# A retention layer with a gated feed-forward on one Trainium2 core: warm-up matmuls recut, the first slices of block 1 reordered, one store per rest pair

## The chip, the core and the metric

The kernel runs on one core of a Trainium2 chip. A core has a matrix engine (TensorE, PE in the profile), a vector engine (VectorE, DVE), a scalar engine (ScalarE, ACT), GpSimd (POOL) and a sync engine (SP). POOL and SP issue the DMA transfers here: POOL all loads, SP all stores and the transposes done by DMA. The metric is device microseconds of one execution, lower is better. The medians below are over several executions.

## What is computed

Eight batches, eight heads, 576 positions, head dimension 64. The attention-like part has no softmax: the score of positions i >= j is multiplied by a decay `gamma_h ** (i - j)`. Its output, 4608 tokens by 512, goes through a two-layer feed-forward with a gated activation:

```python
scores = scale * np.matmul(q, k.transpose(0, 1, 3, 2))
gamma = 1.0 - 2.0 ** (-5.0 - np.arange(H))
Dmat = np.where(rel >= 0, gamma[:, None, None] ** rel[None, :, :], 0.0)
ret = np.matmul(scores * Dmat[None], v)            # 8 x 8 x 576 x 64
x = ret.transpose(0, 2, 1, 3).reshape(B * S, H * D)  # 4608 x 512
h = x @ w_in                                        # 4608 x 2048
g = h * np.clip(h + 3.0, 0.0, 6.0) / 6.0
out = g @ w_out                                     # 4608 x 512
```

## The kernel before

**Pieces and blocks.** The first 512 positions of each batch are cut into four pieces of 128; the last 64 positions of two batches together make a "rest" piece of 128. Pieces are numbered in the order of work: 0 to 3 are batch 0, 4 to 7 batch 1, 8 to 11 batch 2, 12 the first rest piece. The feed-forward works in nine blocks of 512 tokens: block b holds the main positions of batch b, block 8 the four rest pieces. For each piece the kernel makes transposed q and k (`qk`), the masked scores (`at`), the output `o` out of an "inter" part (the state of earlier pieces) and an "intra" part (within the piece), and copies `o` into `xt16` (`intra`, lines 344 to 353). It also updates a running state: `update_mm` on PE (line 355), then `update_state` (line 372), which is two VectorE operations (`ta`, `ts`, lines 383 and 384) and two ScalarE copies of `ts` into `tbd` (lines 394 and 395).

**First layer.** For each of 16 columns fc of `w_in`, `g1` (line 423) takes one of four PSUM banks of the tag `ph`, runs four matmuls of 128x512 into it (line 409), and `g1_act` (line 412) turns it into `gt`: a ScalarE activation into `u` (line 416), then a VectorE operation (line 417) that reads `u` and the bank. The bank is free for column fc + 4 only after that VectorE operation.

**Second layer.** For each 128 tokens mc, `g2` (line 461) runs 16 matmuls into one bank, a ScalarE copy takes it to `osb` (line 471), and `store` (line 450) issues the store on SP. A block of a batch is one transfer of 128 rows; the last block has rows of two batches in each `osb`, and `store` issues two transfers of 64 rows (line 457). The very last 128 tokens go through `g2_halves` (line 474): two halves of 256 columns, each copied by ScalarE (line 484) and stored.

**Order.** Every engine's order is written out by hand. Small operations can be put off in the list `later`; `run_later(n)` issues the first n. `put` (line 583) issues units of feed-forward work, calls `run_later(1)` after each, and then the steps that a table lists for that unit. `gemm1(kb, steps)` does this for the first layer of block kb.

**The start.** While the first loads come in, `warm` (line 170) gives PE matmuls of zeros: 9 of 128x512 at line 178, then in `transposes_early` (line 206) 6 of 128x512 for piece 0, 8 of 128x128 for each of pieces 1 to 3, between the transposes of k and those of q.

**Block 1.** At lines 613 to 618 the first four banks of block 1 are filled in slices of tokens, because the last pieces of batch 1 are still being made. `g1_columns` (line 428) runs tokens 0 to 255 for all four banks; `second_half(7)` makes the output and the state update of piece 7; then tokens 256 to 383 for all four banks, `ahead(8)`, and tokens 384 to 511 for all four banks, each bank's `g1_act` behind its last matmul. `ahead(c)` (line 539) issues the loads up to piece c + 4 on POOL, the DMA transpose of k, one VectorE operation that scales q and v (`vs`, line 306), and the DMA transpose of the scaled q (line 303). `gemm1(1, ...)` then does columns 4 to 15, with `ahead(9)`, `ahead(10)` and `ahead(11)` after columns 6, 9 and 12. The scores of pieces 8 and 9 (lines 316 and 552) follow on PE.

Of the kernel before, what the change touches and what calls it, by code (L numbers as in the profile page):

```python
# [17 lines left out]
def kernel(  # L18
# [16 lines left out]
    nc = tc.nc  # L35
    B, H, S, D = q.shape
    NTOK, DM = out.shape
    DFF = moe_w_in.shape[1]
    P = 128
    NPAIR = H // 2  # L40
    HALF = P // 2
    NCC = DM // P
    NFC = DFF // P
    MBLK = 512
    NMB = NTOK // MBLK
    MAIN = MBLK
# [19 lines left out]
    def column_of(c):  # L66
        kind, b, i, _ = pieces[c]
        return b * MAIN + i * P if kind == "main" else B * MAIN + b * P
# [8 lines left out]
    win16 = big.tile([P, NCC, DFF], FP16)  # L77
    wout16 = big.tile([P, NFC, DM], FP16)
    xt16 = big.tile([P, NCC, NTOK], FP16)
# [90 lines left out]
    def warm(n, cols):  # L170

        w = psum.tile([P, MBLK], FP32, tag="ph", bufs=4, name=f"warm_{warmed[0]}")
        warmed[0] += 1
        for _ in range(n):
            nc.tensor.matmul(w[:, 0:cols], zeros[:, 0:P], zeros[:, 0:cols],
                             start=True, stop=True)

    warm(9, MBLK)

    mask_rest = const.tile([P, P], FP16)  # L180

# [9 lines left out]
    later = []  # L191
# [14 lines left out]
    def transposes_early(c, alone=True):  # L206
        kn, q16 = loaded[c]["kn"], loaded[c]["q16"]
        qk = work.tile([P, 2, NPAIR, P], FP16, tag="qk", bufs=6, name=f"qk_{c}")
        st[c]["qk"] = qk
        pk = psum.tile([P, NPAIR, P], FP16, tag="ph", bufs=4, name=f"trk_{c}")  # L210
        for p in range(NPAIR):
            nc.tensor.transpose(pk[:, p, :], kn[:, 2 * p:2 * p + 2, :], ident16)
        nc.scalar.copy(qk[:, 1], pk)
        if c == 0:
            warm(6, MBLK)
        elif alone:
            warm(8, P)
        pq = psum.tile([P, NPAIR, P], FP32, tag="ph", bufs=4, name=f"trq_{c}")
        for p in range(NPAIR):
            for h2 in range(2):  # L220
                r = slice(h2 * HALF, h2 * HALF + HALF)
                nc.tensor.matmul(pq[r, p, :], q16[:, 2 * p + h2, :], dq[:, 2 * p + h2, :],
                                 start=(p == 0), stop=(p == NPAIR - 1), skip_group_check=True)
        nc.scalar.copy(qk[:, 0], pq)  # L224
        if c == 0:
            warm(8, P)
# [97 lines left out]
    def inter(c, tag="o"):  # L324
        kind, b, i, _ = pieces[c]
        o = psum.tile([P, NPAIR, P], FP32, tag=tag, bufs=4 if tag == "ph" else 1, name=f"o_{c}")
        st[c]["o"] = o
        st[c]["first"] = True
        if kind == "main" and i == 0:
            return  # L330
        qk = st[c]["qk"]
        if kind == "main":
            states = [(st[c].get("before", state_of[b]), slice(0, P))]
        else:
            states = [(state_of[2 * b], slice(0, HALF)), (state_of[2 * b + 1], slice(HALF, P))]
        for j, (state, cols) in enumerate(states):
            for p in range(NPAIR):
                nc.tensor.matmul(o[:, p, cols], tbd[state][:, p, :], qk[:, 0, p, cols],  # L338
                                 start=(j == 0 and p == 0), stop=False, skip_group_check=True)
            if kind == "rest" or st[c].get("last_reader"):  # L340
                free_tbd.append(state)
        st[c]["first"] = False

    def intra(c):
        o, at, vs = st[c]["o"], st[c]["at"], st[c]["vs"]
        for p in range(NPAIR):
            for h2 in range(2):
                r = slice(h2 * HALF, h2 * HALF + HALF)
                nc.tensor.matmul(o[r, p, :], vs[:, 2 * p + h2, :], at[:, h2, p, :],  # L349
                                 start=(st[c]["first"] and p == 0), stop=(p == NPAIR - 1),  # L350
                                 skip_group_check=True)
        g0 = column_of(c)
        nc.scalar.copy(xt16[:, :, g0:g0 + P], o)  # L353

    def update_mm(cs):

        cs = [c for c in cs if pieces[c][0] != "rest"]
        if not cs:
            return
        u = psum.tile([P, len(cs), NPAIR, D], FP32, tag="tu", name=f"u_{cs[0]}")  # L360
        for j, c in enumerate(cs):
            kn, vs = loaded[c]["kn"], st[c]["vs"]
            st[c]["u"] = u[:, j]
            for p in range(NPAIR):
                for h2 in range(2):
                    r = slice(h2 * HALF, h2 * HALF + HALF)
                    nc.tensor.matmul(u[r, j, p, :], kn[:, 2 * p + h2, :], vs[:, 2 * p + h2, :],  # L367
                                     start=(j == 0 and p == 0),
                                     stop=(j == len(cs) - 1 and p == NPAIR - 1),
                                     skip_group_check=True)  # L370
# [26 lines left out]
    def finish(c):  # L397
        intra(c)
        update_mm([c])
        update_state(c)  # L400
        st.pop(c - 2, None)
        loaded.pop(c)
# [9 lines left out]
    def g1_act(kb, ph, fc):  # L412
        if kb not in gts:
            gts[kb] = work.tile([P, NFC, MBLK], FP16, tag="gt16", bufs=2, name=f"gt16_{kb}")
        u = work.tile([P, MBLK], FP32, tag="moeu", bufs=3, name=f"u_{kb}_{fc}")
        nc.scalar.activation(u, ph, ACTF.Relu, bias=cb[:, 0:1], scale=1.0 / 6.0)  # L416
        nc.vector.scalar_tensor_tensor(out=gts[kb][:, fc, :], in0=u, scalar=1.0,  # L417
                                       in1=ph, op0=ALU.min, op1=ALU.mult)

    def g1_bank(kb, fc):  # L420
        return psum.tile([P, MBLK], FP32, tag="ph", bufs=4, name=f"ph_{kb}_{fc}")
# [3 lines left out]
        g1_mm(kb, ph, fc, range(NCC))  # L425
        g1_act(kb, ph, fc)

    def g1_columns(kb, banks, cols):

        t0 = kb * MBLK  # L430
        for fc, ph in enumerate(banks):
            for dmc in range(NCC):
                nc.tensor.matmul(ph[:, cols], win16[:, dmc, P * fc:P * fc + P],
                                 xt16[:, dmc, t0 + cols.start:t0 + cols.stop],
                                 start=(cols.start == 0 and dmc == 0),
                                 stop=(cols.stop == MBLK and dmc == NCC - 1),
                                 skip_group_check=True)
                if dmc == NCC - 1 and cols.stop == MBLK:
                    g1_act(kb, ph, fc)

    def g1_first(kb):

        banks = [g1_bank(kb, fc) for fc in range(2)]
        for dmcs in ((0, 1), (2, 3)):
            for fc in range(2):
                g1_mm(kb, banks[fc], fc, dmcs)
        for fc in range(2):
            g1_act(kb, banks[fc], fc)

    def store(kb, mc, cols, src):  # L450
        if kb < B:
            r0 = kb * S + P * mc
            nc.sync.dma_start(out[r0:r0 + P, cols], src)
        else:
            for i in range(2):
                r0 = (2 * mc + i) * S + MAIN
                nc.sync.dma_start(out[r0:r0 + HALF, cols], src[i * HALF:i * HALF + HALF])

    pouts = {}

# [13 lines left out]
    def g2_halves(kb, mc):  # L474
        gt = gts[kb]
        W = DM // 2
        for half in range(2):
            pout = psum.tile([P, W], FP32, tag="ph", bufs=4, name=f"pout_{kb}_{mc}_{half}")
            for fc in range(NFC):
                nc.tensor.matmul(pout, gt[:, fc, P * mc:P * mc + P],  # L480
                                 wout16[:, fc, half * W:half * W + W],
                                 start=(fc == 0), stop=(fc == NFC - 1))
            osb = work.tile([P, W], FP32, tag="osh", bufs=2, name=f"osb_{kb}_{mc}_{half}")
            nc.scalar.copy(osb, pout)
            store(kb, mc, slice(half * W, half * W + W), osb)


# [37 lines left out]
    def unit1(kb, f0):  # L525
        return lambda: g1(kb, f0)
# [8 lines left out]
    def second_half(c):  # L535
        inter(c)
        finish(c)
# [58 lines left out]
    def gemm1(kb, steps):  # L596

        units = {0: [lambda: g1_first(kb)]}.get(kb, [])
        done = {0: 2, 1: 4}.get(kb, 0)
        put(units + [unit1(kb, f) for f in range(done, NFC)], steps)  # L600
# [10 lines left out]
    run_later(9)  # L611

    banks = [g1_bank(1, fc) for fc in range(4)]
    g1_columns(1, banks, slice(0, 2 * P))
    second_half(7)
    g1_columns(1, banks, slice(2 * P, 3 * P))
    ahead(8)
    g1_columns(1, banks, slice(3 * P, MBLK))
    gts.pop(0)


    gemm1(1, {2: [(ahead, 9)], 5: [(ahead, 10)], 8: [(ahead, 11)]})
    AT = {1: (-1, 7), 4: (-1, 7, 12), 5: (-1, 3, 7, 11)}
    for kb in range(1, NMB - 1):
        mine, next_ = of_block(kb + 1), of_block(kb + 2)
# [45 lines left out]
```

## Time and profile before

| what | value |
|---|---|
| median of 3 runs | 311.14 us (310.1 to 313.22) |
| profiled execution, its own time | 311.39 us |
| its span, first to last instruction | 309.6 us |
| PE busy | 299.5 us, 97% of the span |
| DVE busy | 185.8 us, 60% |
| ACT busy | 173.6 us, 56% |
| POOL busy | 108.0 us, 35% |

The profile is of one execution. Its own time is 1.8 us above its span: that part lies around the first and the last instruction. "Busy" of PE counts pipelined matmuls, so two neighbours overlap; "PEld" is the load of weights. In rows of the timeline the first two numbers are the start and the length in us, and a bracket at the end gives the idle time before and what ended it. A number in ns is the length of one instruction.

### The profile page before, as it was taken

The page shows a single profiled execution, that of the slowest core. Times are in us where ns is not written, and L with a number is a line of the kernel's source. Part 1 is how long each engine was busy: PE and PEld are TensorE (multiplying, and loading weights), DVE is VectorE, ACT ScalarE, POOL GpSimd, SP SyncE. Part 2 cuts the span into 40 slices and gives each one's busy share as a digit, 9 for nine tenths or more (in the row PEclk, how much of TensorE's full clock was granted, in tenths as well). Part 3 has the DMA queues.
Part 4 walks back from the last instruction along what each step waited for, and adds up shares of the span by engine and source line. Part 5 has one row for each costly group of instructions (what it writes and reads, how often), then busy time and mean ns, then how long its engine had stood idle before and what let it go on. Part 6 is the DMA issues. An engine that isn't in the chain of part 4 may idle for free.

```text
span 309.6 us, 5856 instructions
## 1 busy us (share of the span) xinstructions
PE 299.5 (97%) x2286; PEld 152.6 (49%) x2286; DVE 185.8 (60%) x310; ACT 173.6 (56%) x298; POOL 108.0 (35%) x135
## 2 busy tenths in 40 slices
PE   8889999899999999999999999999999999999994
PEld 3644446544544554445544644455445544444443
DVE  4758715796737882885478737856688357207600
ACT  4657356773457554854574737644765467227611
POOL 8974378696735390045353720130000000000000
PEclk9999999999999999999999999999999999999999
DMA  9999999999999999539998996094423230010033
GB/s 65 145 197 190 204 156 211 168 140 156 191 174 170 114 171 163 118 24 154 146 166 74 140 184 138 17 123 69 104 51 53 83 55 0 34 70 34 1 70 68
DMA packets 153164, 35.52 MB, mean 115 GB/s; under 512 B 143792, under 2 KB 148656, under 8 KB 153136
## 3 DMA queue, kind: packets, MB, share of 16 engines
q0 software_dynamic: 117264, 18.36, 82.9%
q1 hardware_dynamic: 35872, 16.79, 27.6%
q8 instruction: 18, 0.29, 0.4%
q14 instruction: 10, 0.08, 0.1%
HBM read 36.70 MB, written 9.44 MB: 149 GB/s over the span
## 4 chain that ended last, share of the span: by engine, by line
PE 76%; DMA 16%; POOL 6%; issue 1%; DVE 0%; ACT 0%; POOLq 0%
PE pout L467 35%; PE ph L409 31%; DMA wout<-in_moe_w_out_dram 5%; POOL qv L91 4%; DMA win<-in_moe_w_in_dram 3%; DMA qv<-in_v_dram 3%; PE o L349 3%; DMA kn<-in_k_dram 3%; DMA qk<-vs 2%; POOL kn L91 2%; PE o L338 2%; PE sc L316 2%; PE u L367 1%; PE pout L480 1%; PE sc L552 1%
## 5 line engine op out<-in xcount | busy, mean ns | idle before, releaser
L417 DVE SCALAR_TENSOR_TENSOR gt<-u,ph 128x512 f16<-128x512 f32 x144 | 98.1, 687 | 69.0 <-ACT u L416 68.3
L467 PE MATMUL pout<-wout,gt 128*128 128x512 f16 x560 | 126.6, 380 | 0.0
L409 PE MATMUL ph<-xt,win 128*128 128x512 f16 x560 | 122.3, 379 | 1.4 <-DVE gt L417 1.4
L416 ACT ACTIVATE u<-ph,cb 128x512 f32<-128x512 f32 x144 | 98.5, 687 | 25.9 <-PE ph L409 25.4
L409 PEld LDWEIGHTS <-win 128*128 128x128 f16 x560 | 54.7, 98 | 67.3 <-issue 1.6
L467 PEld LDWEIGHTS <-gt 128*128 128x128 f16 x560 | 52.3, 98 | 60.8
L91 POOL DMA_DIRECT2D kn<-in_k_dram x40 | 34.4, 861 | 80.9 <-PE u L367 59.2
L471 ACT COPY osb<-pout 128x512 f32<-128x512 f32 x35 | 20.5, 585 | 48.1 <-PE pout L467 47.8
L91 POOL DMA_DIRECT2D qv<-in_q_dram x40 | 34.2, 858 | 7.4 <-DMA wout<-in_moe_w_out_dram 3.0
L320 DVE TENSOR_TENSOR at<-sc,mask_wide 128x1024 f16<-128x1024 f32 x19 | 23.2, 1223 | 22.4 <-PE sc L316 22.4
L91 POOL DMA_DIRECT2D qv<-in_v_dram x40 | 34.6, 868 | 3.2 <-DMA wout<-in_moe_w_out_dram 1.7
L394 ACT COPY tbd<-ts 64x256 f16<-64x256 f16 x28 | 11.3, 405 | 34.1 <-DVE ts L384 17.2
L353 ACT CAST xt<-o 128x512 f16<-128x512 f32 x35 | 19.3, 588 | 10.9 <-PE o L349 10.7
L306 DVE TENSOR_TENSOR vs<-qv,gqv 128x1024 f16<-128x1024 f16 x28 | 17.9, 684 | 0.0
L560 DVE TENSOR_TENSOR at<-sc,mask_wide 128x512 f16<-128x512 f32 x24 | 15.4, 681 | 0.0
L349 PE MATMUL o<-at,vs 128*64 128x128 f16 x280 | 12.2, 223 | 0.0
L395 ACT COPY tbd<-ts 64x256 f16<-64x256 f16 x28 | 11.2, 401 | 0.4
L383 DVE TENSOR_TENSOR ta<-u,ts 128x256 f32<-128x256 f32 x21 | 8.7, 416 | 3.6 <-PE u L367 3.6
L316 PE MATMUL sc<-qk 64*128 64x128 f16 x184 | 9.1, 218 | 1.2 <-ACT qk L224 1.1
L338 PEld LDWEIGHTS <-tbd 128*128 128x128 f16 x124 | 7.9, 98 | 4.5
L384 DVE TENSOR_TENSOR ts<-ta,gc 128x256 f16<-128x256 f32 x21 | 8.9, 425 | 1.7
L349 PEld LDWEIGHTS <-vs 128*64 128x64 f16 x280 | 8.6, 109 | 2.6 <-issue 0.4
(73 smaller groups left out, 120.1 us busy)
## 6 DMA issues: line engine op xcount, KB each, us to landing
out_dram<-osb SPq DMA_DIRECT2D x32, 256.0 KB, 3.5
kn<-in_k_dram POOLq DMA_DIRECT2D x32, 128.0 KB, 6.2
qv<-in_q_dram POOLq DMA_DIRECT2D x32, 128.0 KB, 6.3
qv<-in_v_dram POOLq DMA_DIRECT2D x32, 128.0 KB, 6.5
wout<-in_moe_w_out_dram POOLq DMA_DIRECT2D x4, 512.0 KB, 15.2
win<-in_moe_w_in_dram POOLq DMA_DIRECT2D x3, 512.0 KB, 10.1
out_dram<-osb SPq DMA_DIRECT2D x6, 128.0 KB, 2.3
win<-in_moe_w_in_dram POOLq DMA_DIRECT2D x2, 256.0 KB, 6.2
```

Of the source, the lines that this page charges most:

```text
L91: nc.gpsimd.dma_start(dst[p0:p0 + n], src[b, :, s0:s0 + n, :].rearrange("h s d -> s h d"))
L306: nc.vector.tensor_tensor(out=vs, in0=qv, in1=gqv, op=ALU.mult)
L316: nc.tensor.matmul(sc[:, h2, p, :], qk[r, 1, p, :], qk[r, 0, p, :], start=True, stop=True)
L320: later.append(lambda: nc.vector.tensor_tensor(out=at.rearrange("t a b s -> t (a b) s"), in0=sc.rearrange("t a b s -> t (a b) s"), in1=mas ...
L349: nc.tensor.matmul(o[r, p, :], vs[:, 2 * p + h2, :], at[:, h2, p, :], start=(st[c]["first"] and p == 0), stop=(p == NPAIR - 1), skip_group ...
L353: nc.scalar.copy(xt16[:, :, g0:g0 + P], o)
L409: nc.tensor.matmul(ph, win16[:, dmc, P * fc:P * fc + P], xt16[:, dmc, t0:t0 + MBLK], start=(dmc == 0), stop=(dmc == NCC - 1))
L416: nc.scalar.activation(u, ph, ACTF.Relu, bias=cb[:, 0:1], scale=1.0 / 6.0)
L417: nc.vector.scalar_tensor_tensor(out=gts[kb][:, fc, :], in0=u, scalar=1.0, in1=ph, op0=ALU.min, op1=ALU.mult)
L467: nc.tensor.matmul(pout, gt[:, fc, P * mc:P * mc + P], wout16[:, fc, :], start=(fc == 0), stop=(fc == NFC - 1))
L471: nc.scalar.copy(osb, pout)
L560: nc.vector.tensor_tensor(out=at[:, h2], in0=banks[h2], in1=mask[:, None, :].to_broadcast([P, NPAIR, P]), op=ALU.mult)
```

## The change

Five edits.

1. The zeros at the start: 36 matmuls of 128x128 in place of 9 of 128x512; for piece 0, 24 of 128x128 in place of 6 of 128x512; for pieces 1 to 3, 2 of 128x512 each in place of 8 of 128x128.
2. Block 1: `g1_columns` does one bank. After tokens 0 to 255 of the four banks come `ahead(8)`, then the output of piece 7 and the PE part of its state update; then the third and fourth slices of the banks are interleaved, so that bank 0 ends after 12 matmuls of 128x128, bank 1 after 20, bank 2 after 28, bank 3 after 32. The state update of piece 7 (VectorE and ScalarE) is put into `later`, behind an empty entry: it is issued after column 5.
3. `ahead(9)` comes after column 4 (it was after column 6), `ahead(10)` after column 8 (it was 9); `ahead(11)` stays after column 12.
4. `store` of the last block: one transfer for the two batches, from a view of `out` with the two batches as its first dimension.
5. `g2_halves`: ScalarE copies the left half of each 256 columns and VectorE the right half.

```diff
-    warm(9, MBLK)
+    warm(36, P)
...
         if c == 0:
-            warm(6, MBLK)
+            warm(24, P)
         elif alone:
-            warm(8, P)
+            warm(2, MBLK)
...
-    def g1_columns(kb, banks, cols):
+    def g1_columns(kb, fc, ph, cols):
         t0 = kb * MBLK
-        for fc, ph in enumerate(banks):
-            for dmc in range(NCC):
-                nc.tensor.matmul(ph[:, cols], win16[:, dmc, P * fc:P * fc + P],
...
-                if dmc == NCC - 1 and cols.stop == MBLK:
-                    g1_act(kb, ph, fc)
+        for dmc in range(NCC):
+            nc.tensor.matmul(ph[:, cols], win16[:, dmc, P * fc:P * fc + P],
...
+        if cols.stop == MBLK:
+            g1_act(kb, ph, fc)
...
         else:
-            for i in range(2):
-                r0 = (2 * mc + i) * S + MAIN
-                nc.sync.dma_start(out[r0:r0 + HALF, cols], src[i * HALF:i * HALF + HALF])
+            rests = out.rearrange("(b s) n -> b s n", s=S)[2 * mc:2 * mc + 2, MAIN:S, cols]
+            nc.sync.dma_start(rests, src)
...
-            nc.scalar.copy(osb, pout)
+            nc.scalar.copy(osb[:, 0:W // 2], pout[:, 0:W // 2])
+            nc.vector.tensor_copy(osb[:, W // 2:W], pout[:, W // 2:W])
...
     banks = [g1_bank(1, fc) for fc in range(4)]
-    g1_columns(1, banks, slice(0, 2 * P))
-    second_half(7)
-    g1_columns(1, banks, slice(2 * P, 3 * P))
+    for fc in range(4):
+        g1_columns(1, fc, banks[fc], slice(0, 2 * P))
     ahead(8)
-    g1_columns(1, banks, slice(3 * P, MBLK))
+    inter(7)
+    intra(7)
+    update_mm([7])
+    third, fourth = slice(2 * P, 3 * P), slice(3 * P, MBLK)
+    for fc, cols in ((0, third), (1, third), (0, fourth), (2, third), (1, fourth), (3, third),
+                     (2, fourth), (3, fourth)):
+        g1_columns(1, fc, banks[fc], cols)
+    later.append(lambda: None)
+    later.append(lambda: update_state(7))
     gts.pop(0)
...
-    gemm1(1, {2: [(ahead, 9)], 5: [(ahead, 10)], 8: [(ahead, 11)]})
+    gemm1(1, {0: [(ahead, 9)], 4: [(ahead, 10)], 8: [(ahead, 11)]})
```

In the changed kernel's program, the VectorE copy of each half in `g2_halves` waits for the ScalarE copy of the same half, and the store for the VectorE copy. On PE the order is otherwise the same, on POOL it is the same.

More of the change, by code (lines that the diff above doesn't have):

```diff
@@ L426, in g1 @@
         g1_act(kb, ph, fc)
-    def g1_columns(kb, banks, cols):
+    def g1_columns(kb, fc, ph, cols):
         t0 = kb * MBLK
-        for fc, ph in enumerate(banks):
-            for dmc in range(NCC):
-                nc.tensor.matmul(ph[:, cols], win16[:, dmc, P * fc:P * fc + P],
[L434 to L437, printed above, removed]
-                if dmc == NCC - 1 and cols.stop == MBLK:
-                    g1_act(kb, ph, fc)
+        for dmc in range(NCC):
+            nc.tensor.matmul(ph[:, cols], win16[:, dmc, P * fc:P * fc + P],
+                             xt16[:, dmc, t0 + cols.start:t0 + cols.stop],
+                             start=(cols.start == 0 and dmc == 0),
+                             stop=(cols.stop == MBLK and dmc == NCC - 1),
+                             skip_group_check=True)
+        if cols.stop == MBLK:
+            g1_act(kb, ph, fc)
     def g1_first(kb):
```

## The prediction

> **What bounds the kernel now.** I read the idle time of PE first, since PE is busy for 97% of the span; then a table of stages, to see where its idle time lies; then the timeline there; then the stores at the end, because the changed stores end the program.
>
> PE's five longest waits (engine, line, who was waited for, total, times, longest):
>
> ```profile
> PE ph L409 <- DVE gt L417: 1.4, 1, 1.4
> PE warm L175 <- DVE cb L112: 1.3, 1, 1.3
> PE sc L316 <- ACT qk L224: 1.1, 2, 0.8
> PE trq L222 <- DMA qv<-in_q_dram: 0.9, 1, 0.9
> PE sc L552 <- DMA qk<-vs: 0.6, 1, 0.6
> ```
>
> Only the first and the last lie in block 1. The table of stages (length, busy time of each engine, then granted clock, DMA share, GB/s):
>
> ```profile
> 53.50:59.50 6.00, 4.56 (x73) 4.09 (x70) 4.01 (x8) 3.95 (x9) 4.71 (x7) 1.00 2.21 175
> 59.50:71.30 11.80, 11.16 (x66) 5.06 (x65) 11.09 (x18) 9.18 (x14) 9.55 (x13) 1.00 2.34 144
> 71.30:290.00 218.70, 218.70 (x1622) 108.27 (x1620) 138.19 (x216) 125.93 (x214) 56.00 (x68) 1.00 0.95 104
> 305.40:309.60 4.20, 0.00 (x0) 0.00 (x0) 0.00 (x0) 0.31 (x1) 0.00 (x0) 1.00 0.22 49
> ```
>
> From 71.3 us on PE never stops until 305.3. So the change can only act before 71.3, where at most some 2 us can be had, and after PE's end, where 4.2 us are left that hold one copy and the last stores. In 59.5 to 71.3 DVE is busy 11.09 of 11.80 us: whatever goes to DVE there is nearly on the path. The timeline of block 1:
>
> ```profile
> 56.05 0.58 ACT L353 CAST xt<-o 128x512 f16<-128x512 f32 x1 [0.94 <-PE o L349]
> 57.17 0.40 ACT L394 COPY tbd<-ts 64x256 f16<-64x256 f16 x1 [0.53 <-DVE ts L384]
> 58.01 3.21 ACT L416 ACTIVATE u<-ph,cb 128x512 f32<-128x512 f32 x5
> 58.73 3.21 DVE L417 SCALAR_TENSOR_TENSOR gt<-u,ph 128x512 f16<-128x512 f32 x5 [1.00 <-ACT u L416]
> 59.47 2.75 PE L409 MATMUL ph<-xt,win 128*128 128x512 f16 x12 [1.44 <-DVE gt L417]
> 64.30 1.19 SPq L303 DMA_TRANSPOSE qk<-vs  x1
> 70.96 0.40 PE L552 MATMUL sc<-qk 64*128 64x128 f16 x8 [0.64 <-DMA qk<-vs]
> ```
>
> PE waits at 58 for bank 0: ACT first made the two state copies, then the activation. At 70.3 it waits for the transposed q of piece 9, issued at 64.30. The stores, first those of 128 rows (L453), then those of 64 (L457), with the table of stages over one store of 128 rows, one pair of 64, and the last pair:
>
> ```profile
> L453 SPq DMA_DIRECT2D out_dram<-osb x32: 332/333/1187, 44.3 to 278.3; - x32
> L457 SPq DMA_DIRECT2D out_dram<-osb x10: 466/562/588, 295.5 to 306.2; - x10
> 250.30:251.20 0.90, 0.90 (x6) 0.42 (x5) 0.64 (x1) 0.72 (x2) 0.00 (x0) 1.00 0.77 291
> 296.70:298.15 1.45, 1.45 (x8) 0.67 (x7) 0.00 (x0) 0.00 (x0) 0.00 (x0) 1.00 0.82 181
> 306.85:307.95 1.10, 0.00 (x0) 0.00 (x0) 0.00 (x0) 0.00 (x0) 0.00 (x0) 1.00 0.53 119
> ```
>
> The share is of 16 DMA engines. A store of 128 rows of 2 KB thus takes 0.77 x 0.90 x 16 = 11.1 engine-us, 87 ns a row; the pair of 64 takes 0.82 x 1.45 x 16 = 19.0, 149 ns a row; the last pair 0.53 x 1.10 x 16 = 9.3 for 128 rows of 1 KB, 73 ns. Same rows, same bytes: how a store is dealt out depends on the pattern that it is written in.
>
> **The zeros at the start: 0.** The 9 matmuls of 128x512 start at 1.26 and the next work at 5.07, 427 ns each. The transposes of k behind them have 128 columns and step at (5.50 - 5.07) / 4 = 107 ns, so 36 x 107 = 3.85 us, as 9 x 427 = 3.84. The 24 for piece 0 cost 24 x 57 = 1.37 us (8 at line 175 take 0.62, a step of 57) for 6 x 216 = 1.30: PE then waits for `dq` until 7.1 in any case. The 2 of 128x512 are 0.02 us shorter than 8 of 128x128. Cover: PE waits 0.86 us for q of piece 3 at 16.44, and all before that may grow by as much. If the clock rose later, 24 x 107 = 2.57 us would end 1.2 us later than now, of which ScalarE's constants and this wait hide nearly all. Bounds -0.1 to +0.4.
>
> **Block 1: +0.3.** Up to 56.07 PE has the same order. Then:
> - Bank 0 ends after 12 matmuls, not after 20. Eight take 8 x 56 = 0.45, to 56.52; the next four need `xt` of piece 7, whose cast ends at 56.63, so PE stops 0.18 and bank 0 ends at 56.92, plus 0.17 until the result is seen. ACT starts at 57.11 (before 58.01: the state copies are gone from ahead of it), 0.69; DVE 57.83 to 58.52; column 4 starts at 58.57, not 59.47: 0.90 gained.
> - ACT and DVE step at 0.63 ((3.21 - 0.69) / 4). ACT does columns 0 to 3 at 57.11, 57.74, 58.37, 59.00, column 4 at 59.63, column 5 at 60.48. DVE: column 4 from 60.35, then `vs` of piece 9 (0.65), column 5 from 61.60 to 62.29, and then the moved state update: `ta` 0.44, a step of 0.08, `ts` 0.43, to 63.2. ACT's next instruction behind column 5 is the state copy, which waits for `ts`; queued behind it is the activation of column 6, whose bank was full at 61.3. The copies run 63.25 to 64.09, so column 6 is seen by DVE at 64.8 and its bank is free at 65.5. Column 10 needs that bank and could start at 63.75: a new wait of 1.8 us, charged to DVE `gt` but made by ACT's queue.
> - After it DVE is back to back: columns 6 to 15 and two `vs`. Columns 4 to 15 end at 70.73 (before 69.82: 59.47 + 12 x 0.864 less rounding). Run with the order of before, the same steps give 64.26, 66.85 and 69.44 for the ends of `vs`, which are the trace's.
> - The transpose of scaled q of piece 9 is issued at 61.7, not 64.30. Landing took 6.5 to 8.8 us in this stage, so it is there by 70.5, and the wait of 0.64 at line 552 goes. Late next: the second bank of those scores needs DVE's column 13 (71.2). State matmuls start at 71.55, not 71.29: +0.26. The other moved transposes: k of 9 goes out at 57.4 for 59.06, q of 8 at 56.1 for 57.76, q of 10 and 11 some 0.5 and 0.9 later; they are needed from 78.9 on and the last, issued at 70.6, is there by 79.4 at the latest, so up to 0.3 late. POOL's order, loads included, is the same.
> Bounds: if ACT did not wait, -1.5; with 0.66 a step in place of 0.63, +0.5.
>
> **The copy in halves: 0.** ACT's copies took 372 ns for 256 columns and 585 for 512, so 265 for 128; DVE about 280 by its 687 for 512 and 416 for 256; one behind the other 0.59 with the hand-over, +0.21. It is on the path only if the stores behind it are not late (below).
>
> **One store per rest pair: +11.1.** No transfer in the trace has a first dimension of 2; all begin with 64 or 128 rows. Lower end: it is dealt over 16 engines like the 128-row store, lands in 2.0 to 2.4 us for 2.1 now and is issued 0.3 sooner: -0.3. Upper end: it is dealt by its first dimension, and two engines move 64 rows each. I take the second, because the two forms in the trace already differ by their pattern alone (87 against 149 ns a row, 333 against 562 ns to issue). One engine alone on its rows is nearest to the 128-row form: 87 ns, so 64 x 87 = 5.57 us a store, and 64 x 43 = 2.75 for a half (73 x 87 / 149 = 43). Three pairs and two halves: 3 x 5.57 + 2 x 2.75 = 22.2 us. The pairs come every 3.45 us (295.55, 299.0, 302.4), less than 5.57, so they queue from the first on. Its data starts at 296.74, +0.26 by block 1, and the last row ends at 297.0 + 22.2 = 319.2. Before, the last row ended at 307.94 and the span 1.66 later; so 320.9, +11.3 with the 0.26. Bounds within this case: 70 ns a row if neighbours overlap on an engine, 13.4 + 4.5 = 17.9, span 316.6; 104 ns (8 rows an engine in 0.83 us of the store at 250.36), 27 us, span 325.6.
>
> The Trainium skill, page "DMA: Bandwidth & Descriptors", section "Why a DMA increments its semaphore by 16 and not by 1", says that the number of DMA engines is the largest up to 16 that divides the slowest dimension of both patterns. Here that is 2, against 16 for every store in the trace; the 16 small packets beside each store's rows agree with the 16, and no run here shows the 2. Its figure of about 27 GiB/s per engine would make an estimate of 4.5 us a store, and a sum near 318.
>
> **Sum.** 309.6 + 0.26 + 11.1 = 320.9 of span; with the 1.8 around it 322.7. The profiled execution (311.39) is 0.25 above the median of the runs, so 322.5.
>
> **Rivals.**
> - The stores go over 16 engines (not slower). For: the bytes are those of a store that lands in 2.0 us now. Against: see above. Then block 1's +0.26 and the end's -0.2 (issue 0.3 sooner, copies 0.2 later, one landing for two) cancel: 311.2. It decides from the point where a pair takes under 3.45 us, that is 54 ns a row on two engines: then nothing queues. Chance 0.13.
> - Two engines, but 149 and 73 ns a row, as in the 64-row form: 3 x 9.5 + 2 x 4.7 = 38 us, span 336.7, time 338.2. Against: there 16 engines were busy with 64 rows at a time, here two are. Chance 0.06.
> - 16 engines, and ACT's wait in block 1 does not cost what I say, since column 10 finds its bank free: 309.3. Against: the order on ACT. Chance 0.03.
>
> **How the numbers follow.** Forecast, two engines at 70 to 104 ns a row: 0.78, time 322.5, from 318 to 327.4. I widen to 317.5 and 329 for the spread of the runs (310.1 to 313.22). About 1% is what a measurement of this kernel can tell from no change: slower by more 0.84 (the forecast and the second rival), within 1% 0.14, faster 0.02.
>
> **What would show it.** Right: the rest stores need 10 us and more to land, the DMA share stays near 2/16 from 297 to 319, PE ends near 305.6. In block 1 PE has one wait of about 0.5 us at column 4, one of 1.8 at column 10, and none for a DMA at the scores of piece 9; ACT is idle 2 us before the state copy in between. Wrong: landings of 2 us, or a PE wait anywhere after 71.5.

## The result and the profile after

The changed kernel took 322.11 us (median of 6 runs, 321.62 to 324.38), the kernel before 310.87 us (its median of six runs; the 311.14 in the table above is that of the first three): a ratio of 1.0365, 95% interval 1.0324 to 1.0406, so 11.3 us more (10.1 to 12.6). The forecast was 322.5 us, with a range of 317.5 to 329.

The profiled execution of the changed kernel is the slowest of its six, 324.38 us with a span of 322.6. It lies 2.3 us above the median for a reason of its own, shown below, at the start.

**The end.** First the DMA view from the first rest store's issue to the end, then the groups of instructions on `osb` there, then the table of stages (length, PE, PEld, DVE, ACT, POOL, then granted clock, DMA share, GB/s), over rest pairs 2 and 3 and over the two halves. The DMA share adds up the times of all packets, so packets that overlap can take it over 1:

```profile
DMA  0010111111111111111111111111111111111000
GB/s 0 0 26 26 30 30 46 40 53 53 50 50 53 53 50 50 53 53 50 50 53 53 50 50 53 53 50 50 50 50 48 48 48 48 50 48 48 33 0 0
DMA packets 650, 1.05 MB, mean 42 GB/s; under 512 B 10, under 2 KB 266, under 8 KB 650
```

```profile
L455 SPq DMA_DIRECT2D out_dram<-osb x5: 511/671/4548, 297.9 to 308.3; - x5
L482 ACT COPY osb<-pout x2: 267/267/267, 305.9 to 307.7; 128x128 f32<-128x128 f32 x2
L483 DVE COPY osb<-pout x2: 292/292/292, 306.2 to 308.0; 128x128 f32<-128x128 f32 x2
```

```profile
305.50:315.76 10.26, 2.15 (x20) 1.68 (x18) 0.58 (x2) 0.53 (x2) 0.00 (x0) 0.85 0.13 51
315.76:321.20 5.44, 0.00 (x0) 0.00 (x0) 0.00 (x0) 0.00 (x0) 0.00 (x0) 0.50 0.14 48
```

The compute engines are done by 308.3, and for 13 us the transfer goes on at a share of 0.13 of 16 engines, which is two. Ten packets are under 512 B: two beside each of the five stores, where the kernel before has sixteen beside each. Two pairs take 10.26 us, so 5.13 a pair and 80 ns a row of 2 KB; the halves take 2.72 each, 42.5 ns a row of 1 KB. The first pair is slower: from 299.15 to 302.95 its rows go at 36 GB/s, which is 114 ns a row on each of two engines, and then at 51.

**Block 1.** PE's waits, and the timeline of ACT, DVE and PE around the moved state update:

```profile
PE ph L409 <- DVE gt L417: 1.9, 2, 1.5
PE trq L222 <- DMA qv<-in_q_dram: 1.7, 1, 1.7
PE warm L175 <- DVE cb L112: 1.3, 1, 1.3
PE sc L316 <- ACT qk L224: 1.1, 2, 0.8
```

```profile
58.45 2.12 PE L432 MATMUL ph<-xt,win 128*128 128x128 f16 x32
59.55 3.21 ACT L416 ACTIVATE u<-ph,cb 128x512 f32<-128x512 f32 x5 [0.53 <-PE ph L432]
61.02 5.34 PE L409 MATMUL ph<-xt,win 128*128 128x512 f16 x24 [0.44 <-DVE gt L417]
...
65.51 0.41 ACT L394 COPY tbd<-ts 64x256 f16<-64x256 f16 x1 [1.89 <-DVE ts L384]
66.36 3.21 ACT L416 ACTIVATE u<-ph,cb 128x512 f32<-128x512 f32 x5
67.08 1.88 DVE L417 SCALAR_TENSOR_TENSOR gt<-u,ph 128x512 f16<-128x512 f32 x3 [1.60 <-ACT u L416]
67.82 4.48 PE L409 MATMUL ph<-xt,win 128*128 128x512 f16 x20 [1.46 <-DVE gt L417]
...
73.64 0.44 PE L367 MATMUL u<-vs,kn 128*64 128x64 f16 x16
```

The one wait of 1.44 before column 4 has become two: 0.44 there, and 1.46 six columns later. The wait for the DMA transpose of piece 9 is gone. Read backwards: PE at 67.82 waits for DVE, DVE for ACT (1.60), ACT for DVE's `ts` (1.89). From the third slice to the state matmuls of pieces 8 and 9 PE takes 15.19 us (58.45 to 73.64), before 15.22 (56.07 to 71.29):

```profile
56.07 1.96 PE L433 MATMUL ph<-xt,win 128*128 128x128 f16 x32
71.29 0.44 PE L367 MATMUL u<-vs,kn 128*64 128x64 f16 x16
```

**The start of this execution.** Block 1 begins 2.38 us late. The table of stages, first of the kernel before, then of the changed one:

```profile
12.00:15.00 3.00, 3.00 (x52) 2.28 (x50) 2.52 (x4) 1.75 (x3) 3.00 (x5) 1.00 2.19 145
15.00:19.20 4.20, 3.14 (x52) 2.23 (x50) 2.88 (x5) 1.90 (x4) 4.11 (x6) 1.00 1.40 183
```

```profile
12.00:15.00 3.00, 1.28 (x16) 0.59 (x14) 1.57 (x2) 0.59 (x1) 2.63 (x5) 1.00 2.35 153
15.00:19.20 4.20, 4.20 (x46) 2.46 (x41) 2.58 (x4) 1.76 (x3) 4.20 (x6) 0.59 1.44 190
```

Here the q of piece 2 came later, PE waited 1.7 us for it, and then the granted clock was 0.59 until 19.2. The experiment with the zeros alone, below, bears on whether that belongs to the change.

### The profile page after: what moved, and what is told of

Its sections match the earlier page's. It is cut to its first block, busy times and chain, and to the rows that moved or that the text cites. A ratio compares the mean times of both kernels' runs of the same rounds, so it can differ in the third digit from the quotient of the medians.

```text
span 322.6 us, 5905 instructions
## 1 busy us (share of the span) xinstructions
PE 301.1 (93%) x2313; PEld 155.7 (48%) x2313; DVE 186.1 (58%) x312; ACT 173.2 (54%) x298; POOL 108.0 (33%) x135
## 4 chain that ended last, share of the span: by engine, by line
PE 88%; DMA 2%; POOL 2%; DVE 2%; ACT 1%; issue 1%; ACTq 0%; POOLq 0%
PE pout L465 38%; PE ph L409 36%; PE o L349 3%; PE sc L316 2%; DMA qv<-in_q_dram 2%; PE o L338 2%; PE u L367 1%; PE pout L478 1%; POOL qv L91 1%; PE ph L432 1%; POOL kn L91 1%; PE sc L551 1%; ACT u L416 1%; DVE gt L417 1%; PE trq L222 1%
## 5 line engine op out<-in xcount | busy, mean ns | idle before, releaser
L394 ACT COPY tbd<-ts 64x256 f16<-64x256 f16 x28 | 11.3, 405 | 35.5 <-DVE ts L384 18.6
L353 ACT CAST xt<-o 128x512 f16<-128x512 f32 x35 | 19.3, 588 | 10.9 <-PE o L349 10.7
```

## The experiments

Each was run beside the kernel before on the same chip; ratios are to that kernel, with 95% intervals. The theory: the store's first dimension of 2 puts it on two DMA engines, and all the rest is near 0. Rivals: a store over two batches is slow in whatever order; block 1, the zeros or the split copies carry part of the loss.

**two_stores**, the changed kernel with the old stores:

```diff
-            rests = out.rearrange("(b s) n -> b s n", s=S)[2 * mc:2 * mc + 2, MAIN:S, cols]
-            nc.sync.dma_start(rests, src)
+            for i in range(2):
+                r0 = (2 * mc + i) * S + MAIN
+                nc.sync.dma_start(out[r0:r0 + HALF, cols], src[i * HALF:i * HALF + HALF])
```

> The changed kernel with the two stores of 64 rows per rest pair back in place; all other edits stay. If the first dimension of 2 is the cause (two DMA engines move the whole store), the time falls back by the whole 11 us, to within 1 us of the kernel before, each store's rows end within 1.5 us and land in about 2, and 16 small packets stand beside each store. If block 1 or the zeros carry a part of the loss, that part stays: up to 2.3 us above the kernel before, with PE's end that much later than 305.3.

311.51 us against 310.92, ratio 1.0021 (1.0008 to 1.0034). The loss is gone but for 0.65 us (0.2 to 1.1).

```profile
DMA packets 800, 1.05 MB, mean 73 GB/s; under 512 B 160, under 2 KB 416, under 8 KB 800
out_dram<-osb SPq DMA_DIRECT2D x6, 128.0 KB, 2.3
```

160 small packets beside ten stores are sixteen each.

**one_store**, the same edit the other way: the kernel before, with the new store alone.

> The kernel before with the one store per rest pair alone. If the stores are the cause, +10 to +11.5 us, DMA share 2/16 = 0.125 from about 297 to 319, 2 small packets per store, 80 to 87 ns a row. If the stores only show up together with the late start of the copies (VectorE behind ScalarE), less than +5.

321.32 us against 310.92, ratio 1.0331 (1.0314 to 1.0349): +10.3 us, from this edit alone. The table of stages over two pairs, where the share is 0.13 again:

```profile
302.40:312.60 10.20, 2.11 (x20) 1.64 (x17) 0.00 (x0) 0.74 (x2) 0.00 (x0) 0.86 0.13 51
DMA packets 651, 1.06 MB, mean 43 GB/s; under 512 B 10, under 2 KB 266, under 8 KB 650
```

So the two experiments agree from both sides, and the late VectorE copy is no condition for it.

**rows_first**, the changed kernel, still with one store per pair, but with the rows ahead of the batches. The rows have to lie in that order in `xt16`, so each rest piece takes two ScalarE copies in place of one:

```diff
-            rests = out.rearrange("(b s) n -> b s n", s=S)[2 * mc:2 * mc + 2, MAIN:S, cols]
+            rests = out.rearrange("(b s) n -> s b n", s=S)[MAIN:S, 2 * mc:2 * mc + 2, cols]
...
-        nc.scalar.copy(xt16[:, :, g0:g0 + P], o)
+        to = xt16[:, :, g0:g0 + P]
+        if pieces[c][0] == "rest":
+            for b2 in range(2):
+                nc.scalar.copy(to.rearrange("p c (s b) -> p c s b", b=2)[:, :, :, b2],
+                               o[:, :, b2 * HALF:b2 * HALF + HALF])
+        else:
+            nc.scalar.copy(to, o)
```

> The changed kernel, still with one store per rest pair of the same bytes, but with the 64 rows as the first dimension and the two batches as the second (the rest pieces' tokens are written to xt16 alternating between the batches, which takes two ScalarE copies instead of one per rest piece). If the first dimension decides, 16 small packets per store, landing about 2 us, and the time of the kernel before within 1 us. If one transfer over two batches is slow as such, whatever its order of dimensions, it stays at +10 us.

310.9 us against 310.92, ratio 0.9999 (0.9986 to 1.0011). One transfer, the same bytes, the same two batches; apart from those copies only the order of the dimensions differs.

```profile
DMA  0000990000000198000000009900083000640000
DMA packets 720, 1.05 MB, mean 77 GB/s; under 512 B 80, under 2 KB 336, under 8 KB 720
out_dram<-osb SPq DMA_DIRECT2D x3, 256.0 KB, 2.4
```

```profile
296.10:296.95 0.85, 0.85 (x6) 0.39 (x4) 0.00 (x0) 0.00 (x0) 0.00 (x0) 1.00 0.82 308
```

Sixteen small packets a store; a pair is moved in 0.85 us at a share of 0.82, which is 0.85 x 0.82 x 16 / 128 = 87 ns a row. The rival, that one transfer over two batches is slow in whatever order, falls.

**four_first**, the kernel before with its 64 rows written as 4 x 16 (the rest rows of the output come in another order):

```diff
-                nc.sync.dma_start(out[r0:r0 + HALF, cols], src[i * HALF:i * HALF + HALF])
+                rows = out[r0:r0 + HALF, cols].rearrange("(r a) n -> a r n", a=4)
+                nc.sync.dma_start(rows, src[i * HALF:i * HALF + HALF])
```

> The kernel before with its two stores of 64 rows per pair, each written as 4 x 16 rows that cannot be merged (row 4r + a of the output takes row 16a + r: the rest rows of the output come in another order). If the first dimension is the number of engines, 4 small packets beside each store, 16 rows an engine at 80 to 87 ns = 1.3 to 1.4 us a store; a pair takes 2.7, under the 3.45 between pairs, so nothing queues and the time is +0 to +2 us. If a first dimension under 16 falls to one or two engines whatever it is, 64 rows each or 32, and the time is +10 or more.

313.49 us against 310.92, ratio 1.008 (1.0062 to 1.0098): +2.5 us. The number of engines is as expected, the time is over the range given.

```profile
GB/s 0 0 0 49 44 59 122 88 83 112 98 59 49 49 78 98 83 98 102 63 39 49 78 78 68 68 63 78 102 90 95 90 95 98 59 49 5 0 0 0
DMA packets 681, 1.07 MB, mean 63 GB/s; under 512 B 40, under 2 KB 296, under 8 KB 680
296.40:307.60 11.20, 8.47 (x56) 5.19 (x53) 0.00 (x0) 1.91 (x4) 0.00 (x0) 1.00 0.26 76
```

40 small packets beside ten stores are four each, and a share of 0.26 is four engines. But the rows are slow. The first two pairs take 3.45 and 3.35 us (296.40 to 299.85 to 303.20) where 2.7 were expected, just what lies between two pairs, so these two do not queue yet; the third ends at 307.60, with rows of the first half already among its own, and the half stores behind it end at 310.3, 2.4 us later than the 307.94 of the kernel before.

A row of 2 KB takes some 110 to 117 ns: 11.20 us over 96 rows an engine are 117, but 76 GB/s over 11.20 us are 851 KB, and the six stores have only 786. In the GB/s line (0.42 us a slice) the slow rows are those at the start of each pair: 49, 44, 59; 59, 49, 49; 63, 39, 49. On two engines the first pair began slowly too, at 114 ns a row, and only the queue behind it went at 80. Why the first rows are slow stays open.

**block1_only**, the kernel before with the edits of block 1:

> The kernel before with the edits of block 1 alone (slices interleaved, pieces 8 to 10 transposed sooner, state update of piece 7 after column 5); zeros, stores and last copies as before. By the prediction: PE waits 0.5 us at column 4, 1.5 to 1.8 us at column 10 behind ScalarE's state copy, none for the DMA transpose; the sum is +0.26 us, not to be told from no change. If the shorter wait at column 4 and the sooner transposes are worth more than ScalarE's wait costs, -0.5 us or better.

310.76 us against 310.6, ratio 1.0001 (0.999 to 1.0013). PE's waits are those of the changed kernel, 0.44 and 1.46 us, and none for the transpose.

**late_copies**, which parts the state update in two:

```diff
-        nc.scalar.copy(tbd[new][0:HALF, :, 0:D], ts[0:HALF])
-        nc.scalar.copy(tbd[new][HALF:P, :, D:2 * D], ts[HALF:P])
+        def copies():
+            nc.scalar.copy(tbd[new][0:HALF, :, 0:D], ts[0:HALF])
+            nc.scalar.copy(tbd[new][HALF:P, :, D:2 * D], ts[HALF:P])
+        if copies_later:
+            later.append(copies)
+        else:
+            copies()
...
-    later.append(lambda: update_state(7))
+    later.append(lambda: update_state(7, True))
+    for _ in range(9):
+        later.append(lambda: None)
```

> As block1_only, but the two ScalarE copies of the state of piece 7 are issued after column 15, while the VectorE part stays after column 5. If the new wait at column 10 is made by ScalarE's queue (copy waiting for VectorE, activation behind it), it shrinks from 1.5 to about 0.2 us and the columns end 1.5 us sooner than in block1_only: -1.3 us against the kernel before. If VectorE itself is what column 10 waits for, nothing changes against block1_only.

309.72 us against 310.6, ratio 0.997 (0.9953 to 0.9986): -0.9 us (-1.5 to -0.4), less than the -1.3 expected, though the interval holds it.

```profile
58.03 10.52 PE L416 MATMUL ph<-xt,win 128*128 128x512 f16 x48 [0.44 <-DVE gt L424]
60.81 0.69 ACT L423 ACTIVATE u<-ph,cb 128x512 f32<-128x512 f32 x1 [0.18 <-PE ph L416]
61.13 1.19 SPq L303 DMA_TRANSPOSE qk<-vs  x1
62.41 1.88 DVE L424 SCALAR_TENSOR_TENSOR gt<-u,ph 128x512 f16<-128x512 f32 x3
67.92 2.07 DVE L424 SCALAR_TENSOR_TENSOR gt<-u,ph 128x512 f16<-128x512 f32 x3
69.28 0.40 PE L558 MATMUL sc<-qk 64*128 64x128 f16 x8 [0.40 <-DVE gt L424]
```

The 48 matmuls of columns 4 to 15 run through without a stop: ACT takes column 6 at 60.81, with no state copy ahead of it, and DVE at 62.41. VectorE's part was not moved, so the wait was made by ScalarE's queue. From the third slice to the state matmuls PE takes 14.14 us (55.47 to 69.61), 1.08 less than before; of the 1.46 that went, 0.40 come back at the scores of piece 9.

The profile puts that 0.40 down to DVE, whose column 14 ended just then, at 69.20 (the three at 67.92 are columns 13 to 15). But the scores need column 13, which was done at 68.60, and in **combined**, below, they start at 68.58, before column 14 ends there at 68.87. What came late is the DMA transpose of q of piece 9: issued at 61.13, it landed 8.0 us later, at 69.1, where in block1_only it took 6.9 us. So the wait of the kernel before is back in this execution, and how long that transpose takes to land (7.7 us in combined) is what this stage now hangs on.

**zeros_only**, the three lines of the zeros:

> The kernel before with the zeros at the start cut as in the change, nothing else. By the prediction 0 (-0.1 to +0.4 us): PE's work begins at 5.08 as before and at 7.1 again, and all before the q of piece 3 is hidden. If the fewer, larger zeros for pieces 1 to 3 leave TensorE's clock lower after a wait for q (as in the profiled execution of the changed kernel, where columns of 128 stepped slowly from 15.8 to 19 us), PE's end moves by up to +2.3 us.

310.9 us against 310.6, ratio 0.9999 (0.9983 to 1.0015), and PE's work after the first zeros begins at 5.12 and 7.10 us, before at 5.07 and 7.11. A late q comes with the old zeros too: in halves_only, below, PE waits 1.2 us for one. The late start of the profiled execution is therefore not the work of this edit as a rule; whether the edit makes such a start more likely is open. The other five of the six executions of the changed kernel lie within 0.6 us of each other.

**halves_only**, the split of the last copies:

> The kernel before with the last copies split between ScalarE and VectorE, nothing else. With VectorE's copy behind ScalarE's: 0.27 + 0.03 + 0.29 = 0.59 in place of 0.37 us on the path of the last store, +0.2 us. If the two ran side by side it would be -0.1.

310.87 us against 310.6, ratio 1.0009 (0.9995 to 1.0022), not to be told from no change. In its timeline the two copies stand one behind the other:

```profile
305.60 0.27 ACT L484 COPY osb<-pout 128x128 f32<-128x128 f32 x1 [1.48 <-PE pout L480]
305.90 0.29 DVE L485 COPY osb<-pout 128x128 f32<-128x128 f32 x1 [1.46 <-ACT osb L484]
```

From 305.60 to 306.19 are 0.59 us, where one copy took 0.37: +0.2 us on the path, as worked out, which these runs are too coarse to show.

**combined**, late_copies with the store of rows_first:

> late_copies with the store of rows_first (one store per rest pair, 64 rows first; two ScalarE copies per rest piece); zeros and last copies as before. If the two add, -0.9 us for the late copies and about -0.6 us at the end, since the last store is issued once, 0.5 us sooner, and the 128-row form moves a row in 87 ns for 149: -1.2 to -1.8 us against the kernel before. If the 64-row pairs were hidden but for their issue, -0.9 to -1.2.

308.76 us against 310.55, ratio 0.9953 (0.9934 to 0.9973): -1.5 us (-2.0 to -0.8), as if the two added: -0.9 for the late copies, and some -0.7 for the store, by the ratios of rows_first (0.9999) and two_stores (1.0021). This is faster than both kernels. One of its seven executions took 788.37 us, for which there is no trace and no cause known; the ratio leaves it out.

## Why the prediction was right

- **The store** was forecast at +11.1 us, and measured at +10.3 alone (one_store) and, between the changed kernel (1.0365) and the same one with two stores (1.0021), at some 10.7. Two engines, a queue from the first pair on: as written. That the price of 87 ns a row fits is in part luck: a row takes 80 once the queue runs, 5.13 us a pair for 5.57, and the first pair, with its slow start, took 6.3 us to 305.50; together 16.6 for 16.7. The halves took 2.72 for 2.75. In the profiled execution the last row ends at 321.20, 13.26 after the 307.94 of before; PE's end is 2.35 later, and 10.9 are the store.
- The rule of the Trainium skill, page "DMA: Bandwidth & Descriptors", section "Why a DMA increments its semaphore by 16 and not by 1" (the largest number up to 16 that divides the slowest dimension of both patterns), is borne out by all four forms: 2, 4, 16 and 16 engines. Its figure of about 27 GiB/s for an engine is a little above the measured 2048 B in 80 ns, 23.8 GiB/s.
- **Block 1**: both waits came, at the places named. The new one was forecast at 1.8 us and is 1.46, that at column 4 at 0.53 and is 0.44. Part of this is in the counting: the sum counts from when PE could have started the next matmul, the profile from the end of the last one, which is 0.16 us later (24 matmuls that step at 0.216 us take 5.34; 8 of 128 columns that step at 0.057 take 0.62). That is half of the first difference and more than the second. Column 10 starts 9.37 us after the third slice, for 9.43 in the sum. That the sum of +0.26 is -0.03 in the profile, and nothing in the runs, has another reason: the sum let the second scores wait for DVE's column 13, 15.1 us after the third slice. DVE's columns behind the new wait step at 0.60 to 0.62 us for 0.63, column 13 ended at 14.8, and that wait did not come. ACT was idle 1.89 us before the state copy.
- **The zeros** 0 and **the copies** +0.2 if not covered: the runs of each alone (0.9999 and 1.0009) agree with both, and cannot tell +0.2 from 0. The 0.65 us that two_stores keeps is more than its parts tested alone (0.0, 0.0 and +0.3 us); where the rest lies no run tells. The term that was not in the sum, and lies within the spread of the runs, is the late q of piece 2 with the lower clock after it.

The rivals: 16 engines falls by the ten small packets, 149 ns a row by 80; that column 10 would find its bank free falls by the wait of 1.46.

## What to carry to other kernels

Merging two stores into one saves an issue, but look at the first dimension of the merged pattern before its bytes: put the long dimension first, and count the small packets beside each store and the DMA share in the trace. When an operation is moved out of a wait, look for what stands behind it in its engine's queue; here two copies of 0.4 us, which waited 1.9 for another engine, held up the activation of column 6 by 2.6 (5.34 us after column 4 began, where late_copies has 2.78), and parting the operation so that each engine's piece lies where that engine is free is what gained. A wait that is taken away uncovers the next: of 1.46 us, 0.40 came back as a wait for a transpose. And where the profile names the engine that ended a wait, look at whether the value waited for had not been ready long before: then it was something else, often a DMA.

## What the runs showed of the hardware that was not expected

- Two stores of 64 rows cost 149 ns of an engine per row of 2 KB, one of 128 rows with the same rows 87 ns (rows_first, in the same place of the program). The engines' number is the same, 16.
- With two DMA engines behind, SP itself is held: the last store's issue took 4548 ns, where the others took 511 to 1289.
- On two and on four engines the first rows of a store that queues behind no other are slow: 114 ns a row at the start of the first pair of the changed kernel, 80 later.
- In one execution, a wait of 1.7 us of PE for a load was followed by a granted clock of 0.59 over 4.2 us, although PE was busy throughout these. Waits of 1.1 us (two_stores) and 1.2 us (halves_only) for a load of q at the start were not followed by a lower clock: 1.00 over the 4 us behind them.
